# Seven block products instead of eight in two feed-forward layers, with weights and activations streamed from DRAM

## The chip, the cores and the metric

One NeuronCore of one Trainium2 chip runs the whole program. The metric is the device time of one execution in microseconds (us); lower is better. TensorE (PE) multiplies into PSUM, VectorE (DVE) and ScalarE (ACT) work on PSUM and SBUF, GpSimd (POOL) on SBUF, and SyncE (SP) issues most transfers. Each engine takes its instructions in the order in which the program issues them, and waits on semaphores for the others.

## The reference

For two batches of 3008 tokens with 256 features (6016 tokens in all) it computes

```python
attn = np.maximum(z @ z.T / S, 0.0) ** 2
x = u * (attn @ v)                      # 6016 x 256, float32
h = x @ w_in;  g = h - np.tanh(h);  x = g @ w_out          # network 0
h = x @ w_in2
g = h if h >= 1 else (0 if h <= -1 else (h + 1) ** 2 / 4)
out = g @ w_out2                                           # network 1
```

with `w_in` 256 x 2048 and `w_out` 2048 x 256. The weights arrive as float64, the rest as float32.

## The kernel before

Every product is made of three matmuls on rounded numbers: a float32 operand is split into a high part `hi` (rounded by ACT to the format that PE multiplies) and the rest `lo = x - hi` (DVE), and high x low, low x high and high x high are summed in PSUM.

**Stages.** Attention goes first: 144 steps (two batches, 6 chunks of queries, 12 pairs of key tiles), then network 0 and network 1, each over 12 chunks of 512 tokens (the last has 384) and in each chunk over 8 slices `f` of 256 hidden features. One such step (chunk, f) is 24 matmuls: 12 in `ffn_s` (L378), the first product, with 128x128 blocks of weights against 128x512 of activations (two output halves j, two halves k of the 256 features, three matmuls each, L385 to L387), and 12 in `ffn_av` (L408), the second product (L417; the last chunk of network 1 uses L449 with tokens and weights swapped).

**Between the products** network 0 takes `tanh` on ACT (L394) and subtracts on DVE (L396); network 1 clamps on DVE (L399), squares on ACT (L402) and takes the maximum on DVE (L404). Then `split` (L89) rounds on ACT (L93) and, deferred until the next `flush`, subtracts on DVE (L96). The second product of a step is issued LAG = 2 steps after its first, so PE has two whole steps of other work while DVE and ACT prepare it.

**Weights.** `convert` (L190) turns the 64-bit words of a 256-wide slice of weights into float32 with seven DVE instructions of 512 columns and stores them to a DRAM tile (L221). It is a generator; `make` (L585) advances it by `CONVERT` steps per loop step wherever there is room, with pauses. `load_w` (L173) fetches a slice back and splits it on chip once per network; the 16 split slices then stay in the `ring` (18 buffers) for all 12 chunks. The activations stay on chip, in the `x` tiles; `split_x` (L371) splits a chunk three steps ahead of its use.

**Order.** Everything is under a manual schedule: the main loop (L617) writes out by hand, for each step, loads (`pump`), hooks, the first product of step i, the second product of step i - 2, conversion work, and a tail. PSUM holds two 2-bank score tiles (`ps_s`) and four 1-bank accumulators (`ps_a`); a chunk of a network uses two of the four, so the next chunk starts on the other two.

Of the kernel before, what the change touches and what calls it, by code (L numbers as in the profile page):

```python
# [7 lines left out]
F32 = mybir.dt.float32  # L8
# [11 lines left out]
RING = 18  # L20
AHEAD = 14
UL, UT = 4, 10
QT = 512
CONVERT = (1.5, 2.0)
# [3 lines left out]
def attention_then_two_ffn(  # L28
# [29 lines left out]
    const = ctx.enter_context(tc.tile_pool(name="const", bufs=1))  # L58
    ring = ctx.enter_context(tc.tile_pool(name="ring", bufs=RING))
    cv_p = ctx.enter_context(tc.tile_pool(name="cv", bufs=2))  # L60
    dram_p = ctx.enter_context(tc.tile_pool(name="w32", bufs=1, space=bass.MemoryType.DRAM))
# [6 lines left out]
    ps_s = ctx.enter_context(tc.tile_pool(name="ps_s", bufs=2, space=bass.MemoryType.PSUM))  # L68
    ps_a = ctx.enter_context(tc.tile_pool(name="ps_a", bufs=4, space=bass.MemoryType.PSUM))


    NCH = (NT + 3) // 4
    xs = [
        const.tile([P, 2, P * min(4, NT - 4 * c)], F32, name=f"x{c}") for c in range(NCH)
    ]
# [95 lines left out]
    ws = {}  # L171

    def load_w(key):  # L173
        st = {}
        nm = "_".join(map(str, key))

        def dma():
            r = st["raw"] = raw_p.tile([P, 512], F32, tag="raw", name=f"wraw{nm}")
            nc.sync.dma_start(out=r, in_=w32[key])

        def work():
            w = ring.tile([P, 2, 512], F32R, tag="w", name=f"w{nm}")
            split(w[:, 0, :], w[:, 1, :], st["raw"])
            ws[key] = w

        return [(dma, AHEAD), (work, 1)]

    w32 = {}

    def convert(key, src):  # L190

        nm = "_".join(map(str, key))
        raw = wide_p.tile([P, 1024], U32, tag="wide", name=f"wide{nm}")
        nc.sync.dma_start(out=raw.rearrange("p (k f) -> p k f", k=2), in_=src)
        yield
# [6 lines left out]
        yield  # L204
# [3 lines left out]
        yield  # L208
        nc.vector.tensor_scalar(out=es, in0=ei, scalar1=-896.0 * 2**20, scalar2=0.0, op0=ALU.add, op1=ALU.max)
        yield  # L210
        nc.vector.scalar_tensor_tensor(out=m, in0=low, scalar=2.0**-32, in1=mi, op0=ALU.mult, op1=ALU.add)
        yield
        nc.vector.tensor_scalar(out=es, in0=es, scalar1=255.0 * 2**20, scalar2=8.0, op0=ALU.min, op1=ALU.mult)
        yield
# [3 lines left out]
        yield  # L218
        nc.vector.scalar_tensor_tensor(out=m, in0=m, scalar=2.0**-20, in1=e, op0=ALU.mult, op1=ALU.mult)
        w32[key] = dram_p.tile([P, 512], F32, name=f"w32{nm}")  # L220
        nc.sync.dma_start(out=w32[key], in_=m)  # L221
        yield
# [77 lines left out]
    def attn_av(b, c, t, hi, lo, n):  # L300
# [53 lines left out]
        def scaled():  # L354
            o = 0
            while o < n:
                g, r = divmod(b * S + QT * c + o, 4 * P)
                k = min(n - o, 4 * P - r)
                nc.vector.scalar_tensor_tensor(
                    out=xs[g][:, :, r : r + k], in0=y[:, :, o : o + k], scalar=SCALE, in1=ut[:, :, o : o + k],  # L360
                    op0=ALU.mult, op1=ALU.mult,
                )
                o += k
# [4 lines left out]
    NPF = DFF // (2 * P)  # L368
    xsp = {}

    def split_x(net, c):  # L371
        n = xs[c].shape[2]
        xh = u_p.tile([P, 2, 512], F32R, tag="ub", name=f"xh{net}_{c}")
        xl = u_p.tile([P, 2, 512], F32R, tag="ut", name=f"xl{net}_{c}")
        split(xh[:, :, :n], xl[:, :, :n], xs[c])
        xsp[net, c] = (xh, xl, n)

    def ffn_s(net, c, f):  # L378
        xh, xl, n = xsp[net, c]
        w = ws[net, "in", f].rearrange("p h (k f) -> p h k f", k=2)  # L380
        ps = ps_s.tile([P, 2, 512], F32, tag="s", name="h")
        for j in range(2):
            fs = slice(j * P, (j + 1) * P)
            for k in range(2):
                nc.tensor.matmul(ps[:, j, :n], w[:, 0, k, fs], xl[:, k, :n], start=(k == 0), stop=False)  # L385
                nc.tensor.matmul(ps[:, j, :n], w[:, 1, k, fs], xh[:, k, :n], start=False, stop=False)  # L386
                nc.tensor.matmul(ps[:, j, :n], w[:, 0, k, fs], xh[:, k, :n], start=False, stop=(k == 1))  # L387
# [283 lines left out]
```

## Time and profile before

| | |
|---|---|
| median of 3 runs | 1514.42 us (1514.22 to 1514.76) |
| span of the profiled execution | 1512.6 us |
| median of the runs less that span (what lies around it) | 1.8 us |
| instructions | 21243 |
| PE busy, matmuls | 1507.0 us, 8917 |
| DVE busy | 1077.0 us |
| ACT busy | 818.8 us |
| granted TensorE clock | 1.000 |
| moved by DMA | 56.70 MB |

The span runs from the first to the last instruction of the profiled execution, which is a run of its own beside the three that were timed. A busy time is the sum of an engine's instructions; it doesn't tell whether anybody waited for them. A matmul's duration in the profile covers its passage through the array, and matmuls overlap; what one costs in a row of them is the distance between their starts.

### The profile page before, as it was taken

The numbers are of one execution on the slowest core, as the hardware profiler recorded it, in microseconds if no ns is written. First come the engines' busy times: TensorE is split into PE (matmuls) and PEld (weight loads), VectorE is DVE, ScalarE is ACT, GpSimd is POOL, SyncE is SP. The second block draws the span as 40 slices with busy tenths as digits, with TensorE's granted clock in tenths as the row PEclk, the third lists the DMA queues.
The fourth block names the chain that finished last, engine by engine and source line by source line (L and its number), as shares of the span: only waits on it lengthen the run. The fifth ranks groups of instructions, "written<-read, shape, count | busy, mean of one in ns | idle before, by whom it ended". The sixth has DMA issues, their size and how long they took to land.

```text
span 1512.6 us, 21243 instructions
## 1 busy us (share of the span) xinstructions
PE 1507.0 (100%) x8917; PEld 1279.6 (85%) x8917; DVE 1077.0 (71%) x1142; ACT 818.8 (54%) x867; POOL 0.7 (0%) x5
## 2 busy tenths in 40 slices
PE   9999999999999999999999999999999999999999
PEld 6888888999999888888888888988888888888888
DVE  8888888988888866656644444577776777777675
ACT  8777778877777444444444444454444444344443
POOL 0000000000000000000000000000000000000000
PEclk9999999999999999999999999999999999999999
DMA  7122243222124111011100000010000000000001
GB/s 162 42 56 57 65 95 73 56 53 54 50 57 124 64 42 42 22 42 43 41 16 0 1 1 7 18 46 15 15 1 14 15 15 14 15 14 12 4 15 25
DMA packets 146624, 56.70 MB, mean 37 GB/s; under 512 B 123616, under 2 KB 130144, under 8 KB 146528
## 3 DMA queue, kind: packets, MB, share of 16 engines
q1 hardware_dynamic: 145328, 55.07, 14.7%
q8 instruction: 70, 1.15, 0.3%
q10 hardware_dynamic: 1200, 0.26, 0.1%
q14 instruction: 26, 0.21, 0.1%
HBM read 40.76 MB, written 14.55 MB: 37 GB/s over the span
## 4 chain that ended last, share of the span: by engine, by line
PE 98%; DVE 0%; DMA 0%; ACT 0%; SPq 0%; issue 0%; ACTq 0%; DVEq 0%
PE acc L417 33%; PE acc L311 25%; PE h L385 11%; PE h L387 11%; PE h L386 11%; PE sc L263 6%; PE acc L449 1%; DMA zraw<-in_z_dram 0%; PE acc L328 0%; DVE zt L129 0%; DVE lo L297 0%; DVE a L293 0%; SPq L118 0%; DVE g L404 0%; DVE t L399 0%; DVE gl L96 0%
## 5 line engine op out<-in xcount | busy, mean ns | idle before, releaser
L417 PE MATMUL acc<-gh,w_out 128*128 128x512 f32 (+1 forms) x1472 | 360.3, 387 | 0.0
L93 ACT ACTIVATE gh<-g 128x1024 fp32r<-128x1024 f32 (+1 forms) x192 | 200.4, 1044 | 267.9 <-DVE g L404 141.5
L417 PEld LDWEIGHTS acc<-gh,w_out 128*128 128x128 f32 x1472 | 275.6, 188 | 54.8
L311 PE MATMUL acc<-hi,v 64*128 64x512 f32 (+1 forms) x2256 | 296.2, 383 | 0.0
L385 PE MATMUL h<-xl,w_in 128*128 128x512 f32 (+1 forms) x768 | 295.7, 385 | 0.0
L387 PE MATMUL h<-xh,w_in 128*128 128x512 f32 (+1 forms) x768 | 295.4, 385 | 0.0
L386 PE MATMUL h<-xh,w_in 128*128 128x512 f32 (+1 forms) x768 | 295.4, 385 | 0.0
L96 DVE TENSOR_TENSOR gl<-g,gh 128x1024 fp32r<-128x1024 f32 (+1 forms) x192 | 230.1, 1198 | 68.7 <-ACT gh L93 68.7
L311 PEld LDWEIGHTS acc<-hi,v 64*128 64x128 f32 x2256 | 234.1, 184 | 31.0 <-ACT hi L276 0.8
L396 DVE TENSOR_TENSOR g<-h,t 128x1024 f32<-128x1024 f32 (+1 forms) x96 | 115.4, 1202 | 147.2 <-ACT t L394 147.2
L399 DVE TENSOR_SCALAR t<-h 128x1024 f32<-128x1024 f32 (+1 forms) x96 | 115.4, 1202 | 141.6 <-PE h L387 141.6
L417 PE MATMUL acc<-gl,w_out 128*128 128x512 f32 (+1 forms) x736 | 195.0, 387 | 0.0
L297 DVE TENSOR_TENSOR lo<-a,hi 128x1024 fp32r<-128x1024 f32 (+1 forms) x143 | 170.4, 1199 | 30.7 <-ACT a L291 29.1
L284 ACT ACTIVATE r<-sc 128x1024 f32<-128x1024 f32 (+1 forms) x143 | 144.0, 1007 | 86.6 <-PE sc L263 83.3
L402 ACT ACTIVATE t<-t 128x1024 f32<-128x1024 f32 (+1 forms) x96 | 100.4, 1046 | 156.5 <-DVE t L399 156.5
L394 ACT ACTIVATE t<-h 128x1024 f32<-128x1024 f32 (+1 forms) x96 | 96.8, 1009 | 159.4 <-PE h L387 159.3
L385 PEld LDWEIGHTS h<-xl,w_in 128*128 128x128 f32 x768 | 144.3, 188 | 28.4 <-issue 0.9
L311 PE MATMUL acc<-lo,v 64*128 64x512 f32 (+1 forms) x1104 | 167.1, 383 | 0.6 <-DVE lo L297 0.6
L387 PEld LDWEIGHTS h<-xh,w_in 128*128 128x128 f32 x768 | 144.2, 188 | 27.4
L386 PEld LDWEIGHTS h<-xh,w_in 128*128 128x128 f32 x768 | 144.2, 188 | 27.5
L417 PEld LDWEIGHTS acc<-gl,w_out 128*128 128x128 f32 x736 | 137.8, 188 | 27.4
L287 ACT ACTIVATE hi<-r 128x1024 fp32r<-128x1024 f32 (+1 forms) x143 | 149.3, 1044 | 4.2
(61 smaller groups left out, 1049.2 us busy)
## 6 DMA issues: line engine op xcount, KB each, us to landing
wide_in<-in_moe_w_in_dram SPq DMA_DIRECT2D x16, 512.0 KB, 4.2
wide_out<-in_moe_w_out_dram SPq DMA_DIRECT2D x16, 512.0 KB, 3.8
vraw<-in_v_dram SPq DMA_DIRECT2D x22, 256.0 KB, 3.3
out_dram<-ot SPq DMA_DIRECT2D x88, 64.0 KB, 1.9
ub<-in_u_dram SPq DMA_DIRECT2D x80, 64.0 KB, 2.8
w_in<-m_in SPq DMA_DIRECT2D x16, 256.0 KB, 2.1
w_out<-m_out SPq DMA_DIRECT2D x16, 256.0 KB, 2.1
wraw_in<-w_in SPq DMA_DIRECT2D x16, 256.0 KB, 2.8
```

Source lines behind the costliest of these rows:

```text
L93: nc.scalar.activation(out=hi, in_=src, func=AF.Copy)
L96: nc.vector.tensor_tensor(out=lo, in0=src, in1=hi.bitcast(F32), op=ALU.subtract)
L284: nc.scalar.activation(out=r[s], in_=ps[s], func=AF.Relu)
L287: nc.scalar.activation(out=hi[s], in_=r[s], func=AF.Square)
L297: tail.append(lambda: nc.vector.tensor_tensor(out=lo[s], in0=a[s], in1=hi.bitcast(F32)[s], op=ALU.subtract))
L311: nc.tensor.matmul(acc[d][h][:, :n], lhsT, g[half, j, :n], start=start, stop=stop)
L385: nc.tensor.matmul(ps[:, j, :n], w[:, 0, k, fs], xl[:, k, :n], start=(k == 0), stop=False)
L386: nc.tensor.matmul(ps[:, j, :n], w[:, 1, k, fs], xh[:, k, :n], start=False, stop=False)
L387: nc.tensor.matmul(ps[:, j, :n], w[:, 0, k, fs], xh[:, k, :n], start=False, stop=(k == 1))
L396: nc.vector.tensor_tensor(out=g[s], in0=ps[s], in1=t1[s], op=ALU.subtract)
L399: nc.vector.tensor_scalar(out=t1[s], in0=ps[s], scalar1=1.0, scalar2=-1.0, op0=ALU.min, op1=ALU.max)
L417: nc.tensor.matmul(acc[d][:, :n], w[:, part, j, d * P : (d + 1) * P], g[:, j, :n], start=start, stop=stop)
```

## The change

The first product of a 256-wide slice is a 2x2 block product: weights A11, A21, A12, A22 (128x128 each) against activations of two blocks of features (rows) and two halves of 1024 tokens (columns). The changed kernel forms it with seven block products instead of eight (a Winograd form). For that it prepares sums of weight blocks S1 to S4 (on POOL, once per slice) and differences of activation blocks t1 to t4 (on DVE, once per 1024 tokens), and adds the products up partly in PSUM and partly on DVE.

- The steps become *units* (network, group s of 1024 tokens, f): 6 groups in network 0 (the last of 896 tokens, in halves of 448) and 5 in network 1. A unit has 7 x 3 = 21 matmuls of the first product and 24 of the second product of the unit before. The last 896 tokens of network 1 keep the old eight products (`end_s`, `end_g`, `end_av`).
- A unit takes copies of PSUM by ACT (`snap` m1, u2, u3, and one half of B), sums by DVE (`add`), and works on two halves A and B with the same steps as before (`first`, `square`, `value`, `round`, `rest`).
- Weights are split and summed once, and stored split: `packed`, three 512 KB parts per slice. Each unit streams its three parts back (`load_w`, two units ahead) into a ring of 24 buffers. Attention's output and network 0's output are stored to DRAM (`kept`) and loaded per group.
- `fill` stands at two places of a unit: it takes a step of the next group's activations (`x_steps`, issued from f = 2 on), a transposition of finished output, or conversion work worth `CONVERT[1]` us.
- A group uses all four accumulators; `empty` copies them out behind the first unit of the next group.

Core of the diff (the part of `Unit.emit` whole; `+` omitted where a function is new):

```python
 RING = 18
+SLOTS = 24
-CONVERT = (1.5, 2.0)
+CONVERT = 0.85, 1.4
...
# convert(), after the last DVE step, whose result w is [P, 1024] wide
        def sums():
            for to, x, y, op in ((S1, A21, A22, ALU.add), (S3, A11, A21, ALU.subtract),
                                 (S2, S1, A11, ALU.subtract), (S4, A12, S2, ALU.subtract)):
                nc.gpsimd.tensor_tensor(out=blocks[:, to], in0=blocks[:, x], in1=blocks[:, y], op=op)
...
# load_w(i): three transfers of [P, 1024] float32
        for part in range(3):
            w = ring.tile([P, 1024], F32R, tag="w", name=f"w{i}_{part}")
            nc.sync.dma_start(out=w.bitcast(F32), in_=packed[net, f][:, part, :])
...
# x_steps(net, s): sub and lo on DVE, hi on ACT; two entries are taken per unit
        return load, [
            (sub("t13", 0, b(0, 1), b(0, 0)), hi("b")),
            (sub("t13", 1, b(1, 1), b(0, 1)), None),
            (lo("b", ("b11", "b21")), hi("t13")),
            (sub("t24", 0, b(1, 1), t("t13", 0)), None),
            (lo("t13", ("t1", "t3")), hi("c")),
            (sub("t24", 1, b(1, 0), t("t24", 0)), None),
            (lo("c", ("b22",)), hi("t24")),
            (lo("t24", ("t2", "t4")), None),
        ]
...
# Unit
        def mult(self, bank, block, x, start=False):
            for i, (wp, xp) in enumerate(((0, 1), (1, 0), (0, 0))):
                nc.tensor.matmul(bank[:, : self.w], self.win[wp][:, block, :],
                                 xop[self.net, self.s][x][xp], start=start and i == 0, stop=True, ...)
...
        def emit(self, p, att=None):            # p: the unit before
            Y = self.bank()
            self.mult(Y, A11, "b11", True)
            if p and p.net == 1:
                p.A.round()                     # ACT, 1024 columns
                p.B.first()                     # DVE
            m1 = self.snap("m1", Y)             # ACT, 512 columns
            X = self.bank()
            self.mult(X, A12, "b21", True)
            if p:
                p.A.rest()                      # DVE
                p.B.first() if p.net == 0 else p.B.square()     # ACT
            self.A = Half(self.net, w, "a")
            add(self.A.h[:, 0, :w], m1, X[:, :w])               # DVE, 512
            V = self.bank()
            self.mult(V, S1, "t1", True)
            self.mult(Y, S2, "t2")              # onto Y: after m1
            u2 = self.snap("u2", Y)
            if p:
                p.B.value()                     # DVE
            for fn in one:                      # 8 matmuls of the unit before, A hi
                fn()
            if p:
                p.B.round()                     # ACT
                fill()
            self.mult(Y, S3, "t3")
            u3 = self.snap("u3", Y)
            if p and p.net == 0:
                p.B.rest()
            add(self.A.h[:, 1, :w], u3, V[:, :w])
            if p and p.net == 1:
                p.B.rest()                      # DVE
            for fn in two:                      # 10 matmuls, A lo and B hi
                fn()
            fill()
            if self.net == 1:
                self.A.first()                  # DVE
            self.mult(Y, A22, "t4")
            self.mult(V, S4, "b22")
            self.B = Half(self.net, w, "b")
            if self.net == 0:
                self.A.first()                  # ACT, tanh
                copy(self.B.h[:, 1, :w], Y[:, :w])
                self.A.value()
                add(self.B.h[:, 0, :w], u2, V[:, :w])
            else:
                copy(self.B.h[:, 1, :w], Y[:, :w])              # ACT
                self.A.square()                                 # ACT
                add(self.B.h[:, 0, :w], u2, V[:, :w])           # DVE
                self.A.value()                                  # DVE
            for fn in three:                    # 6 matmuls, B hi and B lo
                fn()
            if self.net == 0:
                self.A.round()
            if p:
                p.empty()                       # only behind f = 7: four copies
...
# end of the main loop
+        for i, (net, s, f) in enumerate(units):
+            if i:
+                load_w(i + 2)
+            if f == 1:
+                ...
+                load_x()
+            elif f == 2:
+                fills.extend(steps)
+            u = Unit(i)
+            u.emit(p, att=(lambda: second(NATT), attention_end) if i == 0 else None)
+            p = u
```

`first` is `tanh` on ACT in network 0 and the clamp on DVE in network 1, now from SBUF to SBUF; `square` is ACT's, `value` DVE's, `round` ACT's rounding to `hi`, `rest` DVE's subtraction to `lo`, all of 1024 columns.

## Rows read from the trace of the kernel before

**Rows 1.** The page: busy time by engine; the chain that ended last, by engine.

```profile
PE 1507.0 (100%) x8917; PEld 1279.6 (85%) x8917; DVE 1077.0 (71%) x1142; ACT 818.8 (54%) x867; POOL 0.7 (0%) x5
...
PE 98%; DVE 0%; DMA 0%; ACT 0%; SPq 0%; issue 0%; ACTq 0%; DVEq 0%
```

**Rows 2.** By stage (attention, network 0, network 1): PE, PEld, DVE, ACT, POOL busy, clock, DMA.

```profile
60.00:480.00 420.00, 420.00 (x3762) 372.47 (x3759) 361.72 (x437) 324.63 (x347) 0.00 (x0) 1.00 0.28 68
500.00:980.00 480.00, 480.00 (x2142) 400.56 (x2141) 270.79 (x282) 209.04 (x220) 0.00 (x0) 1.00 0.07 23
1000.00:1460.00 460.00, 460.00 (x2033) 381.19 (x2032) 331.67 (x294) 193.74 (x189) 0.00 (x0) 1.00 0.07 13
```

**Rows 3.** One step of network 1 in time: start, duration, instruction, idle before.

```profile
1202.49 0.39 PE L385 MATMUL h<-xl,w_in 128*128 128x512 f32 x1
...
1204.99 0.39 PE L387 MATMUL h<-xh,w_in 128*128 128x512 f32 x1
...
1205.41 1.23 DVE L399 TENSOR_SCALAR t<-h 128x1024 f32<-128x1024 f32 x1 [1.80 <-PE h L387]
1206.56 1.22 DVE L96 TENSOR_TENSOR gl<-g,gh 128x1024 fp32r<-128x1024 f32 x1
1206.73 1.06 ACT L402 ACTIVATE t<-t 128x1024 f32<-128x1024 f32 x1 [1.96 <-DVE t L399]
...
1207.83 1.23 DVE L404 TENSOR_TENSOR g<-h,t 128x1024 f32<-128x1024 f32 x1
1207.93 0.39 PE L385 MATMUL h<-xl,w_in 128*128 128x512 f32 x1
...
1209.15 1.06 ACT L93 ACTIVATE gh<-g 128x1024 fp32r<-128x1024 f32 x1 [1.35 <-DVE g L404]
```

**Rows 4.** The timeline in the last chunk (384 tokens): first and twelfth matmul of one first product.

```profile
1495.74 0.34 PE L385 MATMUL h<-xl,w_in 128*128 128x384 f32 x1
...
1497.65 0.33 PE L387 MATMUL h<-xh,w_in 128*128 128x384 f32 x1
```

**Rows 5.** The timeline in network 0: hand-offs from PE to ACT and from DVE to ACT.

```profile
801.45 0.39 PE L387 MATMUL h<-xh,w_in 128*128 128x512 f32 x1
...
801.94 1.03 ACT L394 ACTIVATE t<-h 128x1024 f32<-128x1024 f32 x1 [2.06 <-PE h L387]
803.00 1.22 DVE L396 TENSOR_TENSOR g<-h,t 128x1024 f32<-128x1024 f32 x1 [1.86 <-ACT t L394]
...
804.26 1.06 ACT L93 ACTIVATE gh<-g 128x1024 fp32r<-128x1024 f32 x1 [1.29 <-DVE g L396]
```

**Rows 6.** Groups by line and shape: count, busy us, mean ns of one, idle before.

```profile
L96 DVE TENSOR_TENSOR gl<-g,gh 128x1024 fp32r<-128x1024 f32 x176 | 214.8, 1221 | 61.3 <-ACT gh L93 61.3
L93 ACT ACTIVATE gh<-g 128x1024 fp32r<-128x1024 f32 x176 | 186.9, 1062 | 250.6 <-DVE g L404 132.7 <-DVE g L396 117.9
...
L399 DVE TENSOR_SCALAR t<-h 128x1024 f32<-128x1024 f32 x88 | 107.8, 1225 | 131.0 <-PE h L387 131.0
...
L352 DVE TENSOR_TENSOR y<-y,acc 128x512 f32<-128x512 f32 x20 | 12.9, 681 | 0.0
...
L351 ACT ACTIVATE y<-acc 128x512 f32<-128x512 f32 x20 | 12.0, 600 | 3.5 <-PE acc L311 2.9
...
L203 DVE TENSOR_SCALAR e_in<-wide_in 128x512 uint32<-128x512 uint32 x16 | 6.7, 420 | 0.0
```

**Rows 7.** The timeline: two copies of 448 columns back to back on ACT.

```profile
490.19 0.96 ACT L351 ACTIVATE y<-acc 128x448 f32<-128x448 f32 x2
```

**Rows 8.** The timeline at the end: a weight load that waited for DVE.

```profile
1506.12 0.96 DVE L96 TENSOR_TENSOR gl<-g,gh 128x768 fp32r<-128x768 f32 x1 [0.97 <-ACT gh L93]
...
1507.13 0.30 PEld L449 LDWEIGHTS acc<-w_out,gl 128*128 128x128 f32 x2 [0.33 <-DVE gl L96]
```

**Rows 9.** Windows with transfers: the start, and one of weights alone; last columns DMA share, GB/s.

```profile
0.00:60.00 60.00, 58.08 (x469) 44.42 (x471) 52.09 (x65) 51.11 (x63) 0.73 (x5) 1.00 0.48 108
...
493.20:498.40 5.20, 5.20 (x24) 4.31 (x23) 4.41 (x8) 1.20 (x2) 0.00 (x0) 1.00 0.74 250
```

More of the change, by code (lines that the diff above doesn't have):

```diff
@@ L169, in load_v, with convert @@
         return [(dma, AHEAD), (work, 2)]
[L171 to L194, printed above, removed]
+    NPF = DFF // (2 * P)
+    packed = {
+        (net, f): dram_p.tile([P, 3, 1024], F32, name=f"packed{net}_{f}") for net in range(2) for f in range(NPF)
+    }
+    posts = []
+    done = set()
+    def convert(net, f, which, src):
+        nm = f"{which}{net}_{f}"
         raw = wide_p.tile([P, 1024], U32, tag="wide", name=f"wide{nm}")
         nc.sync.dma_start(out=raw.rearrange("p (k f) -> p k f", k=2), in_=src)
-        yield
+        yield 0.0
         words = raw.rearrange("p (n two) -> p n two", two=2)
@@ L427, in ffn_av @@
                     mm(d, j, 0, lo, stop=(last and j == 1))
[L428 to L431 removed]
+            if last:
                 o = wide_p.tile([P, 2, 16, 32], F32, tag="wide", name="ot")
@@ L638, in attention_then_two_ffn, with attention_end @@
             close()
+        ps_s_guard.__exit__(None, None, None)
+        ps_f = ctx.enter_context(
+            tc.tile_pool(name="ps_f", bufs=4, space=bass.MemoryType.PSUM, reuse_waits="tile")
+        )
+        def attention_end():
+            second(NATT + 1)
+            flush()
+        p = None
+        for i, (net, s, f) in enumerate(units):
+            if i:
+                load_w(i + 2)
+            if f == 1:
+                more = (net, s + 1) if (net, s + 1, 0) in units else (1, 0) if net == 0 else None
+                load_x, steps = x_steps(*more) if more else split_steps()
+                load_x()
+            elif f == 2:
+                fills.extend(steps)
+            u = Unit(i)
+            u.emit(p, att=(lambda: second(NATT), attention_end) if i == 0 else None)
+            p = u
+        load_w(len(units) + 2)
+        one, two, three = p.parts_list
+        nq = 2 * NPF
+        banks = end_s(0)
+        p.A.round()
+        p.B.first()
+        p.A.rest()
+        p.B.square()
+        p.B.value()
+        for fn in one:
+            fn()
+        p.B.round()
+        p.B.rest()
+        held[0] = end_g(0, banks)
+        banks = end_s(1)
+        for fn in two + three:
+            fn()
+        p.empty()
+        held[1] = end_g(1, banks)
+        for q in range(2, nq + 2):
+            if q < nq:
+                if q % 2 == 0:
+                    load_w(len(units) + q // 2 + 2)
+                banks = end_s(q)
+                held[q] = end_g(q, banks)
+                fill()
+            else:
+                flush()
+            end_av(q - 2, *held.pop(q - 2))
 _INS = ["u", "v", "z", "moe_w_in", "moe_w_out", "moe2_w_in", "moe2_w_out"]
```

434 lines of the change are left out of this document (337 added, 97 removed).

## The prediction

> **What bounds the kernel now.** I read the page first: PE is busy 100% of the span, DVE 71%, ACT 54%, and the chain that ended last is PE for 98% [rows 1]. The windows by stage say the same of each stage: PE is busy throughout, at full granted clock, while DVE has idle time: 361.7 us busy of 420 in attention, 270.8 of 480 in network 0, 331.7 of 460 in network 1 [rows 2]. So time is the number of matmuls times their distance. The timeline gives that distance: a step of 24 matmuls starts at 1202.49 and the next at 1207.93, so 5.44 us, 0.2267 us for one of 512 columns [rows 3]. For 384 columns, eleven distances take 1.91 us, 0.174 each [rows 4]; 448 columns, which the trace lacks, I put half way, at 0.200. DVE and ACT prepare the second product two steps (10.9 us) ahead, so no hand-off between them reaches PE today.
>
> **What is removed.** A unit has 45 matmuls where two steps had 48: 45 x 0.2267 = 10.20 us for 10.88. There are 40 such units in network 0 and 40 in network 1: 80 x 0.68 = 54.4 us. The last group of network 0 costs 45 x 0.200 = 9.0 us per slice for 24 x 0.2267 + 24 x 0.174 = 9.6: 8 x 0.6 = 4.8 us. Together 59.2 us, if PE never waits.
>
> **What is added between the products.** Prices: DVE of 1024 columns 1.22, of 512 columns 0.68, ACT 1.06 and 0.60 [rows 6]; an instruction that waits for nothing starts before the one ahead has ended, DVE 0.08 earlier (1205.41 + 1.23 against 1206.56) [rows 3], ACT about 0.1 (two of 0.54 in 0.96) [rows 7], so in a row they cost 1.14, 0.60, 0.96 and 0.50. Hand-offs: ACT to DVE 0.04, DVE to ACT 0.09 [rows 3] or 0.04 [rows 5], 0.07 taken; a matmul's result is with ACT 0.49 after its start [rows 5], which is 0.26 after PE goes on; a weight load follows DVE by 0.05 [rows 8]. The clamp of 1024 columns from SBUF (`first`, network 1) isn't in the trace: from PSUM it takes 1.22, and the only such DVE instruction from SBUF takes 0.42 for 512 [rows 6] against 0.68 for two-input ones. That is 0.27 for 512 columns and 0.15 fixed, so 0.69 for 1024; bounds 0.69 to 1.22, and I take 0.69, because its operands lie as in the nearest row.
>
> By sums nothing overflows. In network 1 a unit has on DVE two maxima and two subtractions, two clamps and three sums, 4 x 1.14 + 2 x 0.61 + 3 x 0.60 = 7.6 us of 10.2, and on ACT 5.8. But the queues are in order and now hand over inside one unit, so I walk the chains.
>
> *Network 0.* With PE at its own pace (clock from the unit's start), S3 ends at 5.21, copy u3 6.07, sum h1 6.79, tanh 7.90, value 9.16, `round` 10.29. The next unit's m1 can't start before 10.20 + 0.68 + 0.26 = 11.14. That leaves 0.8 us, and DVE's conversion work in `fill` fits. Only where a group changes do four copies and the fills push m1 or h1 late, about 1 us a group: 5 us in all. Network 0 gains 32.0 - 5.0 = 27.0 us.
>
> *Network 1.* Here `round` of half A stands in front of m1 on ACT, and S2 must wait for m1, since it adds onto the bank that m1 copies. What is queued behind that wait on PE is the whole rest of the unit. The loop closes: m1 0.60, to PE 0.05, the 27 matmuls from S2 to t4 6.12, to ACT 0.26, copy of B 0.50, `square` 1.06, to DVE 0.04, `value` 1.22, to ACT 0.07, `round` 0.96 (m1 is next). Sum 10.88 us: PE waits 0.68 in each unit, as much as three matmuls are worth. A second loop runs through DVE and ACT alone: `round` 1.10, `rest` 1.14, sum h0 0.60, B's value 1.29, B's round 0.96, u3 0.64, sum h1 0.60, B's rest 1.14, clamp 0.76, square 1.10, value 1.29: 10.62. It has 0.26 to spare, and the fills stand in it: the ACT part of the first fill is ahead of u3, the DVE part of the second is ahead of the clamp (the DVE part of the first falls into DVE's wait for u3, and costs nothing). Per group that is three roundings of 0.96 and one of 0.50, DVE 3 x 0.60 + 1.14, and two transpositions at 0.60: 7.5 us, less 0.26 in six units, 6.0. The four copies of `empty` on ACT (2.0) are covered by `value` but for some 0.7. A group: 8 x 10.88 + 6.7 = 94 us, where 16 steps took 87.0. The first group (no output to transpose, its first unit still at PE's pace) comes to 92, the last (three steps of activations for eight) to 90.5. Sum 3 x 94 + 92 + 90.5 = 464.5 against 80 x 5.44 = 435.2: network 1 loses 29.3 us.
>
> **What else moves.** Conversions: per loop step of attention 0.85 us of DVE for 1.5 instructions of 0.47 on average, 15 us more over some 100 steps. They hide in DVE's 58 idle us there [rows 2]; if that cover were gone, the whole 15 would show. The sums on POOL, 64 of 128 columns in all, run beside attention, where POOL does nothing [rows 2]; no row prices them; from nothing, if nobody waits, to some us where DVE is held up, and I take nothing. The Trainium skill (GPSIMD Engine Reference, 3.1 and Key points) gives 4497 ns for 2048 columns and says that POOL shares its SBUF interfaces with two-input DVE instructions: by it, as an estimate, 64 x 0.28 = 18 us of DVE held, still less than what is left idle; no run here shows it. `load_w` puts 1.57 MB per unit on SP's queue, two units (20 us) ahead of use; at the 250 GB/s of the window of weight traffic [rows 9] that is 6.3 us. Stores of `kept` and output stand ahead of it on SP and wait for DVE or ACT, for at most a unit, inside that lead. The closing part and the start of unit 0 are as before but for some 0.5 us of accumulators to empty.
>
> **Sum.** -27.0 + 29.3 + 0.5 = +2.8 on a span of 1512.6: 1515.4. The runs lie 1.8 us above the span, and I carry that over: **1517 us**, no change within 0.2% (3.0 us, about what a measurement of this kernel can tell from none). Its own range, from hand-offs 0.04 either way in some seven places of each of the 40 units and 0 to 16 us of waits in network 0, is 1505 to 1530.
>
> **Rivals.**
> *PE stays the bound.* The sums of DVE and ACT fit in a unit, and the loop is only 0.68 us too long; if work in network 1 runs ahead by more than I walk, PE keeps its pace. With the loop below 10.2 and the fills still in the chain, 1514.4 - 59.2 + 5 + 30 = 1490; with the fills absorbed too, 1460. For it: DVE's idle time [rows 2]. Against it: each term of the loop is a row, and m1 behind `round` is in the code. Chance 0.29, at about 1475.
> *The clamp is slow.* At 1.22 us for 0.69, half A's clamp makes DVE's loop 0.53 longer: 0.27 net in a unit without fills, 0.53 in one with, about 0.4 over 40 units, +16: 1533; if independent DVE and ACT instructions also fail to overlap by 0.08 to 0.1, +28 more. It decides from a clamp of about 0.95 on, where DVE's loop passes 10.88; in units with fills at once. For it: the only clamp in the trace takes 1.22 [rows 6]; against it: that one reads PSUM. Slower, chance 0.15.
> *The stream is late.* A unit needs 1.57 MB in 10.2 us, 154 GB/s. It decides below that rate: the first 60 us moved 108 [rows 9], at which a unit lasts 14.6 us and the kernel some 300 us longer. For it: that row; against it: that stretch had a DMA share of 0.48, mostly small packets, and the window of weights reached 250. Slower, chance 0.05. The Trainium skill (DMA: Bandwidth & Descriptors, Bandwidth) speaks against the change here: it wants 1 MiB or more per transfer, and between its 0.95 us for 64 KB and 6.15 us for 1 MB a 512 KB part would take 3.4 us, an estimate, three of them in turn 10.1 us, hardly under a unit; the window's 250 GB/s disagrees, and the trace decides.
> *It doesn't do what it says*, and 48 matmuls stay: the listing has 7 x 3; 0.01.
>
> **Numbers.** The forecast has 0.50. Over its range about a quarter lies more than 0.2% below the median (0.13), a third within (0.17), the rest above (0.20). Faster: 0.13 + 0.29 = 0.42; same 0.17; slower 0.20 + 0.15 + 0.05 + 0.01 = 0.41. The range leaves out the best of the first rival (below 1470, 0.10) and the worst of the slow ones (above 1545, 0.09): 1470 to 1545.
>
> **What would show it.** Right: 3 matmuls fewer per unit; network 0's units 10.2 us, network 1's about 10.9 and 11.3 to 12.8 with fills; PE idle in network 1 ahead of S2, released by ACT's m1, some 57 us in all; DVE and ACT each waiting for the other. Wrong: network 1's units at 10.2 us (first rival); a clamp row of 1.2 us (second); PE or ACT released by DMA on `packed` parts (third). Waits of PE in attention would mean that conversions or POOL are not hidden.

## The result, and the profile after

The changed kernel takes 1526.89 us (median of 4 runs, 1522.68 to 1529.52) where the kernel before takes 1514.41 on the same chip: ratio 1.0079, interval 1.0061 to 1.0097, so **0.8% slower**. The forecast was 1517 us, no change, with 1470 to 1545 as its range. The profiled run is the fastest of the four (1522.68 us, span 1520.9); the rows here are its own.

The page, busy time by engine and the chain that ended last, answers to [rows 1]:

```profile
PE 1465.9 (96%) x8653; PEld 1223.2 (80%) x8653; DVE 1264.5 (83%) x1510; ACT 1034.3 (68%) x1249; POOL 54.5 (4%) x69
...
PE 72%; DVE 12%; ACT 9%; issue 5%; DMA 1%; SPq 0%; ACTq 0%; DVEq 0%
```

PE has 41 us less work and a span 8.3 us longer. The chain, 98% PE before, runs through DVE and ACT for 21% now: no single engine is full, and still two of them decide. The windows by stage (attention, network 0, network 1; columns as in [rows 2]) tell where:

```profile
60.00:480.00 420.00, 418.83 (x3756) 362.68 (x3754) 377.94 (x437) 333.85 (x360) 33.41 (x36) 1.00 0.37 104
480.00:970.00 490.00, 486.87 (x2194) 407.64 (x2191) 421.77 (x507) 339.84 (x435) 20.36 (x28) 1.00 0.61 217
970.00:1440.00 470.00, 426.95 (x1831) 341.42 (x1830) 356.51 (x418) 277.00 (x358) 0.00 (x0) 1.00 0.48 161
```

PE is all but full in attention and network 0. In network 1 it is busy 427 us of 470, and DVE only 356.5, ACT 277: a stage in which every engine has room and none gets on. The waits (us in total, times, longest) name the pair:

```profile
ACT hb L493 <- PE m L557: 100.8, 81, 2.6
PEld m L557 <- ACT m L493: 63.8, 42, 2.5
ACT gha L493 <- DVE ta L519: 63.5, 76, 1.4
...
PE m L557 <- ACT m L493: 46.0, 41, 2.1
```

41 waits of PE on ACT's copy `m1` (L493 is `copy`, `m` a bank), one in each unit of network 1 and one in network 0; in turn ACT waits for DVE and for PE.

From the starts of the units in the trace the 8.3 us of span divide like this: attention +2.2 (unit 0 starts at 480.4, where network 0 began at 478.2), network 0 -27.2, network 1 +31.1, the end +2.1.

One plain unit of network 1 (no fills, no new group), from the timeline, runs from 1398.90 to 1409.85, 10.95 us:

```profile
1398.70 1.23 DVE L519 TENSOR_TENSOR ta<-ha,ta 128x1024 f32<-128x1024 f32 x1 [0.27 <-ACT ta L516]
1398.90 0.39 PE L557 MATMUL m<-xlb,w 128*128 128x512 f32 x1
...
1399.96 1.06 ACT L493 ACTIVATE gha<-ta 128x1024 fp32r<-128x1024 f32 x1 [1.29 <-DVE ta L519]
...
1400.49 0.62 PE L557 MATMUL m<-xht,w 128*128 128x512 f32 x2
1400.92 0.58 ACT L493 ACTIVATE m<-m 128x512 f32<-128x512 f32 x1
...
1401.56 0.50 PE L557 MATMUL m<-xlt,w 128*128 128x512 f32 x1 [0.45 <-ACT m L493]
1401.89 0.62 PE L557 MATMUL m<-xht,w 128*128 128x512 f32 x2
...
1408.07 0.60 ACT L493 ACTIVATE hb<-m 128x512 f32<-128x512 f32 x1 [2.35 <-PE m L557]
...
1408.56 1.05 ACT L516 ACTIVATE ta<-ta 128x1024 f32<-128x1024 f32 x1
...
1409.65 1.23 DVE L519 TENSOR_TENSOR ta<-ha,ta 128x1024 f32<-128x1024 f32 x1 [0.27 <-ACT ta L516]
1409.85 0.39 PE L557 MATMUL m<-xlb,w 128*128 128x512 f32 x1
```

This is the loop, closed: half A's value at 1398.70, its `round` at 1399.96 (1.26 later), `m1` behind it at 1400.92 (0.96), S2 on PE at 1401.56 (0.64), 27 matmuls until ACT's copy of B at 1408.07 (6.51), `square` 0.49 later, the next value 1.09 later. Sum 10.95, the unit's length. How to read the wait: the last matmul into the bank of `m1` started at about 1399.36, so by the 0.49 of [rows 5] the bank was ready at 1399.85, a microsecond before ACT took it; the name behind the arrow is ACT, but ACT was held by an instruction that has nothing to do with `m1`. And the idle of 0.45 understates the loss: the matmul before it started at 1400.72, so the next would have started at 1400.95 instead of 1401.56, 0.61 late, and its own distance to the next is 0.33 instead of 0.2267, 0.10 more.

### The profile page after: what moved, and what is told of

Read it like the earlier page. It is cut to its first block, busy times and chain, and to the rows that moved or that the text cites. A ratio compares the mean times of both kernels' runs of the same rounds, so it can differ in the third digit from the quotient of the medians.

```text
span 1520.9 us, 22304 instructions
## 1 busy us (share of the span) xinstructions
PE 1465.9 (96%) x8653; PEld 1223.2 (80%) x8653; DVE 1264.5 (83%) x1510; ACT 1034.3 (68%) x1249; POOL 54.5 (4%) x69
## 4 chain that ended last, share of the span: by engine, by line
PE 72%; DVE 12%; ACT 9%; issue 5%; DMA 1%; SPq 0%; ACTq 0%; DVEq 0%
PE acc L335 24%; PE acc L576 21%; PE m L557 17%; PE sc L287 6%; DVE ta L519 3%; ACT ta L516 3%; PE h L733 3%; DVE ha L496 2%; DVE tb L519 2%; DVE glb L530 2%; ACT gha L493 2%; PE acc L769 1%; PE acc L790 1%; DVE ta L511 1%; ACT u L493 1%
## 5 line engine op out<-in xcount | busy, mean ns | idle before, releaser
L557 PE MATMUL m<-xht,w 128*128 128x512 f32 (+1 forms) x704 | 216.7, 389 | 0.0
L576 PE MATMUL acc<-ghb,w 128*128 128x512 f32 (+1 forms) x704 | 186.5, 387 | 0.0
L557 PE MATMUL m<-xlt,w 128*128 128x512 f32 (+1 forms) x352 | 141.7, 403 | 46.2 <-ACT m L493 46.0
L576 PE MATMUL acc<-gha,w 128*128 128x512 f32 (+1 forms) x704 | 175.2, 392 | 0.0
L576 PEld LDWEIGHTS acc<-gha,w 128*128 128x128 f32 x704 | 133.9, 190 | 27.9
L576 PEld LDWEIGHTS acc<-ghb,w 128*128 128x128 f32 x704 | 132.2, 188 | 25.9
L557 PEld LDWEIGHTS m<-xht,w 128*128 128x128 f32 x704 | 132.8, 189 | 24.4
L493 ACT ACTIVATE gha<-ta 128x1024 fp32r<-128x1024 f32 (+1 forms) x88 | 92.6, 1052 | 64.3 <-DVE ta L519 63.5
L519 DVE TENSOR_TENSOR ta<-ha,ta 128x1024 f32<-128x1024 f32 (+1 forms) x88 | 107.0, 1216 | 32.6 <-ACT ta L516 19.4
L493 ACT ACTIVATE u<-m 128x512 f32<-128x512 f32 (+1 forms) x176 | 103.7, 589 | 43.9 <-PE m L557 38.5
L317 DVE TENSOR_TENSOR a<-r 128x1024 f32<-128x1024 f32 (+1 forms) x95 | 114.9, 1210 | 21.4 <-ACT r L308 19.2
L493 ACT ACTIVATE ghb<-tb 128x1024 fp32r<-128x1024 f32 (+1 forms) x88 | 92.6, 1052 | 47.9 <-DVE tb L519 47.9
L335 PEld LDWEIGHTS acc<-lo,v 64*128 64x128 f32 x1104 | 108.9, 184 | 19.6 <-DVE lo L321 3.2
L493 ACT ACTIVATE hb<-m 128x512 f32<-128x512 f32 (+1 forms) x88 | 52.2, 594 | 102.0 <-PE m L557 100.8
```

Source lines behind the costliest of these rows:

```text
L317: nc.vector.tensor_tensor(out=a[s], in0=r[s], in1=r[s], op=ALU.mult)
L335: nc.tensor.matmul(acc[d][h][:, :n], lhsT, g[half, j, :n], start=start, stop=stop)
L493: nc.scalar.activation(out=out_, in_=in_, func=AF.Copy)
L519: nc.vector.tensor_tensor(out=self.t[self.s], in0=self.h[self.s], in1=self.t[self.s], op=ALU.subtract if self.net == 0 else ALU.max,)
L557: nc.tensor.matmul(bank[:, : self.w], self.win[wp][:, block, :], xop[self.net, self.s][x][xp], start=start and i == 0, stop=True, skip_gro ...
L576: nc.tensor.matmul(self.acc(d, n)[:, : self.w], self.wout[:, part, j, d * P : (d + 1) * P], g[:, at, : self.w], start=start, stop=stop,)
```

## The experiments

Ten kernels. Those with a ratio were run four times and are compared with the kernel before on their own chip (1513.85 to 1514.25 us there); the other four have a single time. One thing disturbs comparisons of a few us: TensorE's granted clock falls for a moment in some executions and not in others, which costs about 1.6 us each time (shown further down). The changed kernel's profiled run has two such falls, one in network 0 and one in network 1; the other profiles have from none to four, and it is said where a comparison hangs on it.

**Is it network 1's seven-product unit?** Network 1 gets its eight products back, in the order of the kernel before (the form that the change keeps for the last 896 tokens), and still streams weights and activations from DRAM; network 0 keeps seven.

```diff
-units = [(net, s, f) for net in range(2) for s in range(NSUP - net) for f in range(NPF)]
+units = [(0, s, f) for s in range(NSUP) for f in range(NPF)]
...
-        nq = 2 * NPF
+        nq = 2 * NPF * NSUP
```

> Network 0 keeps seven products; network 1 goes back to eight block products with the second product two steps behind, and still streams its split weights from DRAM, group by group. Queue theory (network 1 of the changed kernel is slow because DVE and ACT hand over to each other inside one unit, so that PE waits for the copy m1): network 1 is PE-bound again at 5.44 us per step, network 0 keeps its 27 us: 1512.6 - 27 + 2 in attention + 1 to 2 at the seams = 1489 us span, about 1491 us measured, 1.5% under the kernel before. Contention theory (the 158 GB/s of streamed weights and activations slow the engines): the stream is still there in network 1, so its steps last longer than 5.44 us and the time stays above 1505 us. Load theory (DVE's busy time in network 1 is the bound): as the queue theory here, since DVE has less to do with eight products.

Measured 1491.43 us (1490.3 to 1492.07), ratio 0.9849 (0.9834 to 0.9864); span 1488.5. Page of this kernel:

```profile
PE 1476.7 (99%) x8773; PEld 1249.5 (84%) x8773; DVE 1232.8 (83%) x1520; ACT 935.0 (63%) x1059; POOL 54.7 (4%) x69
```

120 matmuls more and 35 us less (32 us of span in the profiled runs, some 3 of them the two falls of the clock, which this one hasn't). There is no wait of PE in network 1 any more. So the streams, which this kernel keeps, cost nothing that shows, network 0's part is a gain, and the loss sits in network 1's units.

**Is it the order of the queues, or the amount of work?** Three instructions of network 1 are issued earlier, none is added or taken away: half A's clamp ahead of the older B's `rest`, A's `square` ahead of the copy of B, A's value ahead of the sum into B.

```diff
             add(self.A.h[:, 1, :w], u3, V[:, :w])
+            if self.net == 1:
+                self.A.first()
             if p and p.net == 1:
                 p.B.rest()
...
-            if self.net == 1:
-                self.A.first()
             self.mult(Y, A22, "t4")
...
             else:
-                copy(self.B.h[:, 1, :w], Y[:, :w])
                 self.A.square()
-                add(self.B.h[:, 0, :w], u2, V[:, :w])
+                copy(self.B.h[:, 1, :w], Y[:, :w])
                 self.A.value()
+                add(self.B.h[:, 0, :w], u2, V[:, :w])
```

> The changed kernel with the same work, and three instructions of network 1 moved in their queues: half A's clamp ahead of half B's rest on DVE, half A's square ahead of the copy of B on ACT, half A's value ahead of the sum of B on DVE. Queue theory: the loop through m1 becomes shorter than 10.2 us and only the fills still delay it; walked with the rows' durations a group takes 85 to 86 us for 93.4, so 5 x 8 = 39 us less: span near 1482 us, about 1485 us measured. Contention theory and load theory: neither work nor traffic has changed, so 1521 to 1528 us as before the move.

Measured 1488.89 us (1488.1 to 1489.04), ratio 0.9831 (0.9815 to 0.9848), span 1487.2. Waits of PE in network 1:

```profile
PE m L557 <- ACT m L493: 7.7, 10, 1.2
PE acc L576 <- DVE glb L530: 2.6, 12, 0.2
```

The same instructions in another order make the median 38 us shorter. Network 1 alone takes 431 us for 465 from start to start of its units, 34 less, and more than the 31 that it had lost; 1.6 of the 34 are the fall of the clock in network 1. From the second group on plain units last 10.2 us, PE's own pace; it is the order. The median is 4 us above the 1485 expected: units with fills last 11.1 us and those behind a change of group 11.4, so that groups take 86.5 to 86.8 for the 85 to 86 walked. The three moves were not tried one by one.

**Is it `m1` behind `round` alone?** `m1` goes ahead of the older A's `round`; nothing else.

```diff
+            m1 = self.snap("m1", Y)
             if p and p.net == 1:
                 p.A.round()
                 p.B.first()
-            m1 = self.snap("m1", Y)
```

> The changed kernel with one move: in network 1 the copy m1 stands ahead of half A's round on ACT (and half B's clamp behind both). If the place of m1 behind round were the whole cause, PE's wait of 0.7 us and more in each of 40 units would go: 1490 to 1495 us. Queue theory with two loops: the second loop, round, rest, value, round, rest, clamp, square, value on DVE and ACT alone (10.6 us, with fills up to 12.5), takes over at once: 0 to 0.5 us per group, so units without fills at 10.7 to 10.9 us, units with fills as they were, span 1517 to 1521 us. Contention theory and load theory: no change.

Measured 1518.47 us, span 1516.7, plain units 10.79 to 10.82. Waits of PE in network 1:

```profile
PE acc L576 <- ACT ghb L493: 14.2, 39, 0.5
PE acc L576 <- ACT gha L493: 12.6, 17, 0.9
PE m L557 <- ACT m L493: 1.7, 3, 1.2
```

The wait that the waits view named is gone, 42 of 44 us in network 1, and 4.2 us of span come back, 1.6 of them because the clock didn't fall in network 1. Other waits stand in its place: PE now waits for the roundings `gha` and `ghb`, at 10.8 us per unit. One plain unit in the timeline:

```profile
1395.85 0.60 ACT L493 ACTIVATE m<-m 128x512 f32<-128x512 f32 x1 [1.08 <-PE m L557]
1396.34 1.05 ACT L493 ACTIVATE gha<-ta 128x1024 fp32r<-128x1024 f32 x1
...
1397.43 1.23 DVE L530 TENSOR_TENSOR gla<-ta,gha 128x1024 fp32r<-128x1024 f32 x1 [0.80 <-ACT gha L493]
1398.57 0.68 DVE L496 TENSOR_TENSOR ha<-m,m 128x512 f32<-128x512 f32 x1
1399.17 1.22 DVE L519 TENSOR_TENSOR tb<-hb,tb 128x1024 f32<-128x1024 f32 x1
...
1400.42 1.06 ACT L493 ACTIVATE ghb<-tb 128x1024 fp32r<-128x1024 f32 x1 [1.59 <-DVE tb L519]
...
1401.54 1.65 PE L576 MATMUL acc<-ghb,w 128*128 128x512 f32 x6 [0.28 <-ACT ghb L493]
```

This is another loop, through all three engines: `m1`, A's `round` behind it, A's `rest`, the sum h0, B's value, B's round, PE's wait for it, and 21 matmuls later the next `m1` at 1406.64, 10.79 us after the last. It isn't the second loop of the forecast's walk (10.62, through DVE and ACT alone), which has some 0.25 to spare here: A's value is ready at 1396.03, and `round` starts at 1396.34, behind `m1`. That one binds in most units with fills, where `round` starts 0.03 behind the value. Loops of nearly one length hide each other: removing the first alone brings almost nothing.

**What do the fills cost?** The preparation of network 1's activations is left out for groups 1 to 4 (they reuse group 0's, so those outputs are not the reference's).

```diff
-                load_x, steps = x_steps(*more) if more else split_steps()
-                load_x()
+                if more and net == 1:
+                    xop[more], steps = xop[1, 0], []
+                else:
+                    load_x, steps = x_steps(*more) if more else split_steps()
+                    load_x()
```

> The changed kernel without the preparation of network 1's activations for its groups 1 to 4 (no load, differences or splits; they multiply group 0's operands again), so the fills there hold only the transpositions of output. Queue theory: what stood in the loop goes, 1.3 + 1.3 + 0.9 + 1.9 us = 5.4 us in four groups, 21 to 22 us: units without transposition all at 10.9 us, span near 1499 us; PE still waits 0.7 us a unit for m1. Load theory: DVE has 5.8 us less per group, 23 us in all, and the remaining wait scales with DVE's load. Contention theory: 5 MB of 240 less, no change that can be seen.

Measured 1500.76 us, span 1498.9. Groups take 87.9 to 89.1 us where they took 92.4 to 95.3, plain units still 10.95. So this preparation costs 4.6 to 4.9 us of a group (6.2 in one, where the clock fell). With the 1.2 us that remain in a group for the transpositions and the change of group (88.8 for 8 x 10.95), fills and change cost 5.8 to 6.1 us a group, where the forecast had 6.7, beside the 0.75 of every unit. Of the 22 us of span, some 3 are the two falls of the clock, which this profile hasn't.

**The fills moved, alone.** In network 1 both fills go between the copy `u3` and the sum `h1`, where DVE waits for ACT anyway.

```diff
                 p.B.round()
-                fill()
+                if self.net == 0:
+                    fill()
             self.mult(Y, S3, "t3")
             u3 = self.snap("u3", Y)
+            if self.net == 1:
+                fill()
+                fill()
...
-            fill()
+            if self.net == 0:
+                fill()
```

> The changed kernel with only the fills of network 1 moved, both between u3 and h1, and none of the three moves. Queue theory: units without fills stay at 10.9 us, since their loops are as before; units with activation steps fall from 12.0 to 12.6 to about 11.5 us: 3.5 us a group, span about 1504 us. If the three moves alone were the cause, and the fills' place were indifferent: 1519 to 1523 us.

Measured 1505.18 us, span 1503.4: 17.5 us under the changed kernel's profiled run, some 3 of them the two falls of the clock, which this profile hasn't. Most units with fills are down to the plain 10.95; two per group, at 11.8 to 11.9, and the one behind a change of group are not.

**Moves and fills together.**

> The changed kernel with the three moves of the run before, and in network 1 both fills between the copy u3 and the sum h1 (no longer between round and u3, and no longer ahead of the clamp). Same instructions, same traffic. Queue theory: neither loop reaches 10.2 us any more, walked with the rows' durations every unit of network 1 lasts 10.2 us: 5 x 81.6 = 408 us for 465, so span 1520.9 - 57 = 1464 us, about 1466 us measured, 3.2% under the kernel before. Contention theory or load theory (DVE busy 76% of network 1): PE's waits stay, at or above the 1487 us of the three moves.

Measured 1479.62 us (1477.86 to 1479.79), ratio 0.9769 (0.9754 to 0.9783), span 1477.8: 2.3% faster than the kernel before, and 14 us slower than expected. From the second group of network 1 on all units last 10.2 us except two in each group, 11.82 and 11.4. The one of 11.82 in the timeline, with the last two steps of the activations as its fills:

```profile
1118.78 0.60 ACT L493 ACTIVATE u<-m 128x512 f32<-128x512 f32 x1 [0.38 <-PE m L557]
1119.27 1.05 ACT L452 ACTIVATE xht<-t 128x1024 fp32r<-128x1024 f32 x1
...
1120.36 1.23 DVE L468 TENSOR_TENSOR xlt<-t,xht 128x1024 fp32r<-128x1024 f32 x1 [2.45 <-ACT xht L452]
...
1121.50 0.68 DVE L496 TENSOR_TENSOR ha<-u,m 128x512 f32<-128x512 f32 x1
...
1122.23 0.96 PE L557 MATMUL m<-xhc,w 128*128 128x512 f32 x3 [0.61 <-DVE ha L496]
```

`u3` is copied by 1119.4, yet the sum `ha` starts at 1121.50: DVE stands in `xlt`, which waits for ACT to round the same numbers. PE waits for that sum, since it needs the bank V again. In the unit after a change of group four copies of accumulators stand on ACT ahead of `round` and `m1`.

**Those two stalls taken away.** The last subtraction goes into the next unit, and two of the four copies go to DVE, as in network 0.

```diff
             (lo("c", ("b22",)), hi("t24")),
+            *[(None, None)] * (net == 1),
             (lo("t24", ("t2", "t4")), None),
...
-                    if d and self.net == 0:
+                    if d:
```

> The three moves and the moved fills, with two edits more, both in network 1: the last subtraction of the activations' preparation a unit later, so that DVE does not wait for ACT's rounding of the same numbers in one unit, and two of the four copies of accumulators on DVE instead of ACT. If the 14 us by which the kernel with moved fills missed were these two units of each group (11.82 and 11.4 for 10.2), then all units of network 1 last 10.2 to 10.4 us, groups 82 to 83, and the time is 1479.6 - 12 = 1466 to 1469. If those long units were instead a sum of small delays which the queues only show there, the waits turn up in the neighbouring units and the time stays at 1474 to 1480.

Measured **1469.88 us** (1469.79 to 1471.44), ratio 0.9709 (0.9692 to 0.9725), span 1469.6 in the profiled run: 2.9% faster than the kernel before, 57 us faster than the changed one. Groups of network 1 last 81.8 to 81.9 us (the first 83.6; in the last one unit of 11.82 remains), where 16 steps of the kernel before took 87.0. The time is 1 us above what was expected. The page:

```profile
PE 1454.4 (99%) x8653; PEld 1235.2 (84%) x8653; DVE 1272.5 (87%) x1520; ACT 1032.3 (70%) x1239; POOL 54.5 (4%) x69
...
PE 96%; DVE 2%; ACT 1%; issue 1%; SPq 0%; DMA 0%; ACTq 0%; DVEq 0%
```

DVE is busier than in the changed kernel, 87% for 83%, and PE is the chain again.

**The ends of the stages.** To the moved kernel: no conversion beside unit 0 of network 0 (its successor lasted 14.5 us), and the last two stores issued by ACT.

```diff
-            if self.net == 0:
+            if self.net == 0 and not att:
                 fill()
...
-                nc.sync.dma_start(out=to[:, t0 : t0 + k, :], in_=o[:, t0 : t0 + k, :])
+            parts.append((t0, k))
+        for t0, k in reversed(parts):
+            nc.scalar.dma_start(out=to[:, t0 : t0 + k, :], in_=o[:, t0 : t0 + k, :])
```

> The order of e5_order, and two seams: no conversion work in unit 0 (where half A's value stood behind two conversion instructions, and PE waited 2.4 us for m1), and the last two stores of the output both issued by ACT instead of one behind eight others on SP. Expected against e5_order: 1.0 us less at the start of network 0 (up to 2.7 us if the clock no longer falls there) and 2.0 us less at the end: span about 1461 us. If the end is set by the landing of the eight stores and not by the queue they are issued from, only the first part.

Measured 1478.8 us (1478.48 to 1479.77), ratio 0.9765 (0.9749 to 0.9782): the same as without, where 3 us less had been expected. The unit came down from 14.54 to 11.98, some 1.6 of it because the clock didn't fall there. But attention ended 0.7 us later in this profile, and other units of network 0 and the first of network 1 took the rest back; and the stretch after network 1's units kept its 89 us.

**The last eight stores over two queues**, on top of the two stalls' kernel.

```diff
-    def out_tiles(tok, o):
+    def out_tiles(tok, o, spread=False):
...
-                nc.sync.dma_start(
+                (nc.scalar if spread and h else nc.sync).dma_start(
                     out=out[tok : tok + QT, d : d + 32].rearrange("(c a) e -> a c e", a=32),
...
-                out_tiles(2 * QT * LAST, o)
+                out_tiles(2 * QT * LAST, o, True)
```

> As the kernel before it in this list, and of the last eight 64 KB stores four issued by ACT, four by SP. If these issues one after the other on SP (4.2 us) set the end, the stretch from the end of network 1's units to the end of the span gets 1 to 2 us shorter; if the closing products set it, nothing changes (within 0.3 us).

Measured 1470.15 us (1469.44 to 1471.61), ratio 0.9712 (0.9697 to 0.9726). Its profile has

```profile
1461.05 2.02 SPq L539 DMA_DIRECT2D out_dram<-ot  x4
1461.65 2.09 ACTq L539 DMA_DIRECT2D out_dram<-ot  x4
...
1463.82 0.40 SPq L830 DMA_DIRECT2D out_dram<-o  x1
1463.94 0.38 ACT L826 ACTIVATE o<-acc 128x256 f32<-128x256 f32 x1 [4.54 <-DMA out_dram<-ot]
```

The issues take 2 us instead of 4 to 5, and from the last matmul of network 1's last unit to the end of the span it is 78.8 us for 79.6. But ACT, which now issues four of them, comes to its last copy only behind them, and the time is the same. Less than the 1 to 2 us expected, and not to be told from nothing.

**Do POOL's sums hold up DVE?** They are replaced by one copy on DVE (the sums S1 to S4 are left out).

```diff
-            for to, x, y, op in ((S1, A21, A22, ALU.add), ...):
-                nc.gpsimd.tensor_tensor(out=blocks[:, to], in0=blocks[:, x], in1=blocks[:, y], op=op)
+            nc.vector.tensor_copy(out=w[:, 512:], in_=w[:, :512])
```

> The changed kernel without the sums S1 to S4 on POOL: a DVE copy of 512 columns fills their place (it leaves out the weight sums). Attention ended 2.2 us later in the changed kernel than in the one before. If POOL's 54 us beside DVE are the cause, attention is back to the kernel before within 0.5 us, and the conversion's first instructions fall from 0.46 to 0.42 us; if the conversion work itself is (85 us of DVE for some 70 before, 15 us of roundings on ACT), attention keeps its 2.2 us. Network 0 and network 1 unchanged in either case: span 1518 to 1521 us.

Measured 1525.77 us, span 1524.0, for the 1518 to 1521 expected: no gain. The 3 us above the changed kernel's profiled run are two more falls of the clock, four for two. Unit 0 starts at 480.67 where it started at 480.41, so no sign that attention lost its 2.2 us to POOL; the test is not a clean one, since the copy put in costs DVE 16 x 0.42 us over the whole run. It does hold DVE, only under cover; the groups by line and shape, of the changed kernel first (count, busy us, mean ns of one, idle before), then of this one:

```profile
L511 DVE TENSOR_SCALAR ta<-ha 128x1024 f32<-128x1024 f32 x40 | 27.2, 680 | 0.0
...
L226 POOL TENSOR_TENSOR win<-win 128x128 f32<-128x128 f32 x64 | 53.8, 859 | 857.5 <-DVE win L214 856.3
...
L197 DVE TENSOR_SCALAR eout<-wideout 128x512 uint32<-128x512 uint32 x16 | 8.5, 529 | 0.0
```

```profile
L197 DVE TENSOR_SCALAR eout<-wideout 128x512 uint32<-128x512 uint32 x16 | 6.7, 421 | 0.0
```

The instruction that DVE issues while POOL adds takes 529 ns on average, 421 without POOL.

## Why the prediction was right or wrong

The forecast of the likeliest time was 1517 and the measured one 1526.89: inside its range, the mechanism as walked, the sign of the small difference missed (it had put 0.17 on no change and 0.41 on slower).

- *Matmuls saved.* Right. 45 for 48; units of network 0 last 10.20 us, as worked out. The price for 448 columns, put half way at 0.200, is 9.12 / 45 = 0.2027.
- *Network 0, -27.0.* Measured -27.2, by other means, so that the sum came out is luck: most changes of group cost next to nothing (groups are mostly 81.6, which is 8 x 10.2), and 4.3 of the 5 us put there are in one place, unit 1, at 14.5 us. There attention's closing sums and a piece of conversion stood on DVE ahead of half A's value, so `round` and `m1` behind it were late on ACT and PE waited 1.99 us; the rest is a fall of the clock. In three of the ten profiles with this order (eight products in network 1, no preparation, the fills alone) PE waits as long, the clock stays at 1.00, and the unit lasts 12.9. With the conversion out of the way it took 11.98.
- *Network 1, +29.3.* The loop was named with its every term. The plain unit is 10.95 for 10.88, the rest mostly in one term: the matmuls from S2 to the copy of B took 6.51 for 6.38, since the first behind a wait is 0.10 longer. Groups 92.4, 93.4, 93.7, 95.3 and 90.4 for 92, 94, 94, 94 and 90.5: 465.2 for 464.5, and the excess over PE's own 408 us is 57.2, for "some 57". The experiments on order, on `m1` and on the fills show each part: the first loop (the wait goes with `m1` moved), and fills and changes of group, 5.8 to 6.1 us a group for 6.7. What the walk lacked is the loop that binds plain units once `m1` is moved, at 10.79, through PE's wait for `ghb`; the second loop that it had, 10.62, shows only in units with fills.
- *The clamp.* 680 and 686 ns for 0.69 taken: the second rival falls, by these rows.
- *PE stays the bound.* Falls for this kernel as issued. With the three moves plain units run at PE's pace, and 1488.89 is close to the 1490 that this rival gave with the fills still in the chain; with moved fills and the two stalls gone it is 1469.88, for 1460. So the rival was wrong about the order and right about the sums of work.
- *The stream.* Not late: no wait of PE on `packed` parts anywhere. While 512 KB transfers, weight parts and others, stood in a row on SP's queue, they moved at 397 to 422 GB/s (windows below, from 496 on), well over the 250 assumed; at that rate three take 3.9 us for 6.3. The Trainium skill (DMA: Bandwidth & Descriptors, Bandwidth) had by its sizes, an estimate, given 10.1 us for the three; that does not hold where they follow one another on one queue, and the trace decides.
- *POOL.* Nothing on the path, as taken, though the price was off: the Trainium skill (GPSIMD Engine Reference, 3.1) had led to 0.28 us per sum of 128 columns, the rows show 0.86 on average. Its Key points name as contending with POOL the DVE instructions with two SBUF inputs and those in a 2-port perf mode; here a one-input one is the slower for it (529 ns for 421), and no run shows in which mode it was.
- *Attention, taken as hidden.* Wrong by a little: +2.2 us in the profiled run (over the eleven profiles of the changed kernel and its variants unit 0 starts at 479.5 to 480.7, so 1.4 to 2.5 us behind the kernel before's 478.2). The conversions are DVE's 16 us more in that window (377.94 for 361.72 [rows 2]), nearly all covered; PE's waits for DVE's `lo` there grew from 0.6 to 1.7 us in the view of waits. That the denser conversions are their cause was not tried.
- *The end, +0.5.* Measured +2.1. The last two chunks of tokens now alternate, so eight 64 KB stores of the one stand on SP in front of the last store of the other. That is in the timeline; the attempts to shorten it moved the time by nothing that can be told.

Where the time was missed, the weak step is the last of the sum: one span for all runs, with the clock at its full level throughout as before. The 1.8 us carried over held (1522.68 over a span of 1520.9, 1529.52 over 1527.7), but the spans now differ: the profiled run is 4.2 us under its own median, because TensorE's clock now falls. In windows of 1 us from 494 (busy by engine, then clock, DMA share, GB/s):

```profile
494.00:495.00 1.00, 0.00 (x0) 0.00 (x0) 0.47 (x2) 1.00 (x3) 0.00 (x0) 1.00 1.31 169
495.00:496.00 1.00, 0.89 (x2) 0.74 (x3) 1.00 (x2) 1.00 (x2) 0.00 (x0) 0.62 0.73 217
496.00:497.00 1.00, 1.00 (x4) 0.76 (x3) 1.00 (x2) 0.30 (x2) 0.00 (x0) 0.50 1.05 397
497.00:498.00 1.00, 1.00 (x4) 0.81 (x3) 0.97 (x3) 0.70 (x2) 0.00 (x0) 0.50 1.01 410
498.00:499.00 1.00, 1.00 (x4) 0.76 (x4) 0.97 (x2) 0.66 (x1) 0.00 (x0) 0.67 1.03 422
499.00:500.00 1.00, 1.00 (x7) 0.81 (x6) 1.00 (x2) 0.00 (x0) 0.50 (x1) 1.00 1.01 414
```

After PE's wait of 2 us the granted clock is 0.50, that is 1.2 GHz of 2.4, until 498.7; the shortfalls add up to 0.38 + 0.50 + 0.50 + 0.33 = 1.7 us. It happened once more, at 1331.5, behind a wait of 2.1 us, and made that group 95.3 us. The four runs have mean clocks of 0.997, 0.993, 0.993 and 0.996 and spans of 1520.9, 1527.7, 1527.1 and 1523.1: 0.004 of 1521 us is 6 us, about what the slower two lack. That those runs' falls lie at the same kind of wait was not seen, since they have no trace. But the kernel without POOL's sums, whose network 1 is the same, has a clock of 0.995 and three falls there, each at most 1.6 us after a wait of 2.1 us in the unit with the last steps of the activations: these three units last 14.2 us, the fourth of the kind, without a fall, 12.6. In sum, of the 12.5 us by which the median lies above before, the forecast had 2.8; attention 2.2, the end 1.6 and network 1 1.8, less 0.2 in network 0, make the profiled run's 8.3, and 4.2 are most likely the clock in the other runs. The 1.8 of network 1 are 1.6 for the one fall and 1.1 because the kernel before took 434.1 us there and not 435.2, less 0.9 by which the groups were otherwise shorter than walked.

## What to carry to other kernels

When a change saves work on the bound engine and hands results over inside one unit of work where they had two, walk each in-order queue around the loop and add up its terms before counting busy time: here every engine had room and the unit was still 0.75 us too long. Look for the next-longest loops at once, those through PE too, because removing the wait that the profile names only uncovers them. Here the same instructions in another order turned 0.8% slower into 2.3% faster, and with two copies given to another engine and one subtraction issued later into 2.9%. A step that needs another engine's result for numbers of its own should not be issued right behind that result's maker, in front of something the bound engine needs.

## What the runs showed of the hardware that was not expected

- Stalls of PE can cost more than their length: two of the changed kernel's waits, of 2.0 and 2.1 us, were each followed by a stretch at 1.2 GHz that lost 1.7 us. Others as long were not: the distance between matmul starts was 2.38 and 2.49 us at those two, and 2.51, 2.51, 2.51 and 2.46 us at 1037.1, 1141.5, 1235.2 and 1388.1, where the granted clock stayed at 1.00. In the kernel without POOL's sums three gaps of 2.51 us were followed by such a stretch and a fourth was not; so a wait of this length doesn't tell by itself whether the clock falls. The four runs of the changed kernel spread by 0.45%, those of the kernel before by 0.04%.
- The first matmul behind a wait takes 0.34 us to its successor, not 0.2267 (39 of the 40 such waits in network 1 of the changed kernel; the one at half clock 0.55).
- POOL's sum of two 128x128 float32 blocks took 859 ns on average by the rows (the four sums of a slice 3.67 to 3.99 us together), five times DVE's 0.68 us for 512 columns when counted per column, and DVE's one-input instruction beside it 529 instead of 421.
- 512 KB transfers in a row on one queue reached 397 to 422 GB/s.
